# Short convolution with eight time steps by sixteen channels on the partitions

## The chip, the cores and the metric

The kernel runs on one core of a Trainium2 chip. The core has a matrix engine (TensorE, PE in the profile; PEld is its weight load), a vector engine (DVE), a scalar engine (ACT), GpSimd (POOL), a sync engine (SP) that issues most transfers, and 16 DMA engines. TensorE writes only to PSUM, and only DVE and ACT read PSUM here. The metric is the device time of one execution in microseconds; less is better.

## What is computed

Sequence length 2048, width 640, bf16 inputs. A block with a layer norm, a short convolution with four taps, a long convolution by FFT and a gate, and then a second layer norm with an MLP:

```python
k_shift = sum(k_pad[:, t:t + S, :] * shift_k[:, ks - 1 - t] for t in range(4))
kv = k_shift * v
y = irfft(rfft(kv, 2 * S) * rfft(ssm_k, 2 * S))[:S] + kv * ssm_D
h = x + layernorm(x) * y
out = h + mish(layernorm(h) @ w1 + b1) @ w2
```

## The kernel before

Each step of the work is an operation with a name, an engine (or a choice of two), operations that it depends on, and PSUM tiles that it fills or uses. The text `ORDER` (L26 on) lists all 660 names. Every engine issues its operations in the order of that list and waits only for what they depend on; `:d`, `:a` or `:p` puts an operation on DVE, ACT or POOL where it has a choice (ACT is the default for most evictions), and `@0` to `@3` gives the matmul groups one of four PSUM slots of 1024 float32 columns. A group can only start when the slot's last user has been evicted.

Channels come in five blocks m (0 to 4) of 128, in which channel = 20 d + 4 m + l, with d of 32 and l of 4. Stages, by name:

- `d_n`, `dadd`, `k1pe`, `k1ev`: load the long filter, add the skip term at time 0, transpose it 16 steps at a time.
- `s1kpe`, `s1kev`: first stage of the filter's transform, 20 pieces of 16 matmuls (L399, L400), each evicted with 1024 columns. `s2kpe`, `s2kev` (L425 with 160 columns): second stage, 22 pieces of 6 matmuls (the last of 2), which need every `s1kev` and their piece of the table (`d_g`). `sw` (L453): ten DMAs that swap partitions of the result; they need all `s2kev`.
- Short convolution. k is loaded with 16 consecutive time steps in a partition (128 partitions). `ktpe` (L344) transposes it as float32 words, which hold two channels each: 40 transposes give tiles whose partitions are 4 time steps by 32 d, for four groups of time steps. `ktev` copies them to SBUF (`kt_s`), `ktsh` (L348, POOL) makes a copy of the last group shifted by one partition of time, so that the first group can see the 16 steps before. `kspe` (L360, L361): ten groups (m, half h of the time groups) of 16 matmuls. For each l and time group, L360 multiplies the tile with a 128 x 128 banded weight, and L361 adds the reach-over: the time group before it, into the first 96 columns, since three of the four time steps of a group need taps from the group before. `kv` (L365, DVE) multiplies by v.
- The weights of that convolution: `cfpe` (L307) repeats the taps over the partitions, `coef` (L312, four casts) writes them shifted by the time step, `wsh0` to `wsh3` (L320, POOL) multiply them with a mask, five of the 20 (m, l) pairs in each, 224 columns a pair.
- `s1vpe`/`s1vev`, `s2v*pe`/`s2v*ev`: the same two stages for kv (20 pieces, then 20 pieces of L425 with 64 or 32 columns). `pr` (L464, DVE): the products in frequency. `i1pe`/`i1ev` (L485): first inverse stage, 20 pieces. `i2` (L537), `y`: second inverse stage, 16 tiles t of 128 tokens, evicted by `y`.
- `ln1`, `ln1p`, `lnx`: first layer norm of a tile (DVE statistics, POOL, then POOL or ACT). `wb`, `h`: gate and residual. `bn`, `pow`, `hc`: second layer norm. `tr` (DMA transposes, L579) or `trpe`/`trev` for the first two tiles: the normalised tile, transposed.
- MLP in five units of 2, 2, 4, 4 and 4 tiles: `m1pe` (L604, L611), `hb` (ACT, Mish), `m2pe` (L669, L677), `res` (DVE), `d_out`.

Lines L264 and L266 are the helper that all evictions go through, on ACT and on DVE.

Of the kernel before, what the change touches and what calls it, by code (L numbers as in the profile page):

```python
# [27 lines left out]
s1kpe0_3@3 k1ev1 s1kpe0_1@0 s1kev0_3 d_k1 s1kpe0_0@1 dadd2 s1kev0_1 s1kpe1_3@2 s1kev0_0:d dadd3:p d_g4 s1kpe0_2@3 k1pe2@0 s1kev0_2 dadd4:p d_g1  # L28
s1kev1_3 kz b1pe@1 k1pe4@3 k1ev2 c_b1 cfpe@2 k1pe3@1 k1ev4:a coef d_v0 s1kpe2_0@0 k1ev3 wsh1 s1kpe2_1@2 s1kev2_0 s1kpe4_3@3 d_g7 s1kev2_1:d s1kpe3_1@1
s1kev4_3 s1kpe2_2@0 wsh3 s1kpe1_0@2 s1kev3_1 d_v1 s1kev2_2:d s1kpe4_1@3 d_g2 s1kev1_0 s1kpe3_2@1 s1kev4_1:d s1kpe1_2@0 s1kev3_2 d_g6 ktpe0_0@2 wsh2  # L30
ktpe0_3 ktpe0_2 s1kev1_2 ktpe2_0@3 ktpe2_3 ktpe2_2 d_v2 ktpe2_1 ktpe0_1 ktev2 ktpe1_0@1 ktev0:a ktpe1_1 ktpe1_3 ktpe1_2 s1kpe3_3@0 d_g5 ktev1 ktsh2
s1kpe4_0@3 s1kev3_3 s1kpe1_1@2 ktsh0 s1kev4_0:d d_v3 s1kpe4_2@1 wsh0 s1kev1_1 s1kpe3_0@0 s1kev4_2:d s1kpe2_3@3 s1kev3_0 d_g3 ktpe4_0@2 ktpe4_2 ktpe4_3
s1kev2_3 ktsh1 ktpe3_0@1 ktpe4_1 ktpe3_3 ktev4 ktpe3_1 ktpe3_2 s2kpe_6@0 s2kpe_12@3 ktev3 s2kev_6 kspe0_0@2 s2kev_12 s2kpe_18@0 kv0_0 ktsh3 kspe2_0@1
s2kev_18 ktsh4 s2kpe_42@3 kv2_0 kspe3_0@2 s2kev_42 s2kpe_96@0 kv3_0 s2kpe_24@1 s2kev_96 kspe4_0@3 s2kev_24 kspe1_0@2 kv4_0 s2kpe_108@0 kspe1_1@1 kv1_0
s2kev_108 s2kpe_72@3 kspe0_1@0 d_x1 s2kev_72 kv1_1 d_x0 s2kpe_66@2 s2kpe_102@3 s2kev_66 kv0_1 kspe4_1@1 s2kev_102 s2kpe_120@2 kv4_1 kspe3_1@0
# [3 lines left out]
s1vpe0_3@1 s1vev1_2 s1vpe1_3@0 s1vev0_3:d s1vpe0_1@2 s1vev1_3 s1vpe3_0@3 s1vev0_1:d s1vpe4_1@1 s1vev3_0 s2kpe_30@0 s1vev4_1:d s2v0pe_0@2 s2kev_30
s2v0pe_48@3 s2v0ev_0 ln1_1 sw1_0 s1vpe2_0@1 s2v0pe_64@0 sw1_1 s2v0ev_48 lnx0:p s1vev2_0:d s2v0pe_112@2 sw0_0 ln1p1 s2v0ev_64 sw4_0 s2v0pe_32@3  # L40
s2v0ev_112:d s2v0pe_80@1 sw3_1 s2v0ev_32 s1vpe3_1@0 lnx1:p sw0_1 ln1_2 s1vpe4_0@2 s2v0ev_80 sw3_0 s1vpe3_3@3 sw4_1 ln1_3 s1vev3_1 ln1p2 s1vpe2_3@1
sw2_0 s1vev4_0 s1vev3_3:d sw2_1 s1vpe4_2@0 lnx2:p s1vev4_2 s2v0pe_96@3 pr1_64 ln1p3 s2v0pe_16@2 s2v0ev_96 s2v2pe_32@0 s1vev2_3:d lnx3:p s2v0ev_16
# [130 lines left out]
def kernel(  # L173
# [28 lines left out]
    cst = cpool.tile([P, 3 * P + 32], BF16, name="cst")  # L202
# [537 lines left out]
```

## Time and profile before

| what | value |
|---|---|
| median of 3 runs (lowest to highest) | 222.93 us (222.92 to 223.5) |
| profiled execution, its own time | 223.02 us |
| its span in the profile | 221.2 us |
| granted clock of TensorE | 0.999 |
| PE busy | 212.5 us, 96% |
| DVE, ACT, POOL busy | 137.6, 127.9, 62.0 us |

The span runs from the first to the last instruction; the profiled execution's own time has 1.8 us around it. In the timeline a line has a start, a length, the engine, the source line, the operation, output and input and a count of merged instructions; the brackets at the end give the idle time before it and what ended it. The chain of waits is followed back from the last instruction.

### The profile page before, as it was taken

Reading aid. Unit: us, or ns where it says so; the run is one execution under the profiler, and the core shown is the slowest. Engines: PE = TensorE matmul, PEld = TensorE weight load, DVE = VectorE, ACT = ScalarE, POOL = GpSimd, SP = SyncE. Lnnn points to the kernel's source line nnn. Section 1 sums busy time; section 2 is a strip of 40 time slices with the busy share of each in tenths; the row PEclk is TensorE's granted clock in tenths of the full one; section 3 lists DMA queues with packets and bytes.
Section 4 is the critical chain, followed back from the end, with each engine's and each line's share of the span. In section 5 each row is a group of like instructions: output and inputs, shape, how many; then the busy total and the mean of one; then the engine's idle time right before and its main releaser. Section 6 shows DMA issues by size and latency. Waiting matters only on the chain.

```text
span 221.2 us, 6309 instructions
## 1 busy us (share of the span) xinstructions
PE 212.5 (96%) x2740; PEld 156.0 (71%) x2746; DVE 137.6 (62%) x236; ACT 127.9 (58%) x175; POOL 62.0 (28%) x123
## 2 busy tenths in 40 slices
PE   7899999999879999999999999999999999999994
PEld 2899999898769998578867644444567445667663
DVE  2776899999999999899998679920002200002223
ACT  2389888999999999899753038426600257020000
POOL 5147620011870002147988655320000000000000
PEclk9999999999999999999999999999999999999999
DMA  5999994462992690833004402552001100000204
GB/s 168 393 408 416 407 403 109 166 205 87 410 409 92 207 384 9 276 127 77 0 1 27 94 0 59 124 119 59 0 3 59 59 0 3 0 0 3 89 0 148
DMA packets 19564, 30.98 MB, mean 140 GB/s; under 512 B 10705, under 2 KB 14929, under 8 KB 18769
## 3 DMA queue, kind: packets, MB, share of 16 engines
q1 hardware_dynamic: 19104, 30.46, 40.0%
q8 instruction: 21, 0.34, 0.6%
q10 hardware_dynamic: 336, 0.12, 0.2%
q14 instruction: 7, 0.05, 0.1%
q0 software_dynamic: 96, 0.00, 0.0%
HBM read 20.42 MB, written 2.62 MB: 104 GB/s over the span
## 4 chain that ended last, share of the span: by engine, by line
PE 72%; ACT 12%; DVE 6%; DMA 5%; issue 2%; SPq 1%; DVEq 0%; ACTq 0%
PE ps L669 26%; PE ps L604 26%; ACT uv L264 9%; PE ps L537 3%; DMA ks<-ks 3%; PE ps L399 3%; PE ps L425 3%; DMA ks<-in_A_ssm_k_dram 3%; PE ps L344 2%; PE ps L379 2%; DVE ks L266 2%; ACT ks L264 2%; PE ps L360 2%; DVE ra L365 1%; DVE uv L266 1%
## 5 line engine op out<-in xcount | busy, mean ns | idle before, releaser
L626 ACT ACTIVATE ks<-ps,b1s 128x512 bf16<-128x512 f32 (+1 forms) x69 | 36.2, 599 | 44.1 <-PE ps L604 35.1
L669 PE MATMUL ps<-ks 128*128 128x320 bf16 (+2 forms) x420 | 58.6, 299 | 0.0
L604 PE MATMUL ps<-G 128*128 128x512 bf16 (+1 forms) x319 | 57.2, 336 | 0.3
L669 PEld LDWEIGHTS <-ks 128*128 128x128 bf16 x420 | 40.6, 98 | 17.4 <-issue 1.3
L694 DVE TENSOR_TENSOR rb<-ps,rb 128x640 bf16<-128x640 f32 x15 | 11.8, 817 | 64.5 <-PE ps L677 52.2
L604 PEld LDWEIGHTS <-G 128*128 128x128 bf16 x325 | 31.4, 98 | 24.3 <-issue 1.1
L264 ACT CAST ks<-ps 128x960 bf16<-128x960 f32 (+3 forms) x48 | 39.3, 896 | 8.3 <-PE ps L400 5.0
L264 ACT CAST uv<-ps 128x1024 bf16<-128x1024 f32 x46 | 42.6, 1157 | 0.5 <-PE ps L485 0.4
L464 DVE TENSOR_TENSOR ks<-ks,uv 128x2048 bf16<-128x2048 bf16 x20 | 23.4, 1236 | 0.2 <-DMA ks<-ks 0.2
L425 PEld LDWEIGHTS <-G 128*128 128x128 bf16 x512 | 21.0, 96 | 3.1 <-issue 2.5
L485 PE MATMUL ps<-a_t,ks 128*128 128x128 bf16 (+1 forms) x416 | 17.1, 208 | 0.4
L485 PEld LDWEIGHTS <-ks 128*128 128x128 bf16 (+1 forms) x416 | 16.5, 114 | 1.0 <-issue 0.4
L266 DVE CAST uv<-ps 128x1024 bf16<-128x1024 f32 x14 | 16.4, 1210 | 0.2
L530 POOL TENSOR_SCALAR ra<-rb,r,nmr 128x640 bf16<-128x640 bf16 x11 | 12.5, 1133 | 9.9 <-PE ps L400 9.3
L425 PE MATMUL ps<-uv,G 128*128 128x64 bf16 (+1 forms) x384 | 12.9, 187 | 1.7 <-ACT uv L264 1.5
L550 DVE BATCH_NORM_STATS2 st<-rb 128x6 f32<-128x320 bf16 x32 | 14.0, 479 | 0.1
L516 DVE BATCH_NORM_STATS2 st<-rb 128x6 f32<-128x320 bf16 x32 | 13.7, 469 | 0.0
L365 DVE TENSOR_TENSOR ra<-ps,rb 128x1024 bf16<-128x1024 f32 x10 | 11.9, 1222 | 0.7 <-PE ps L361 0.5
L266 DVE CAST ks<-ps 128x1024 bf16<-128x1024 f32 (+2 forms) x10 | 11.3, 1160 | 1.0 <-PE ps L537 0.6
L528 ACT ACTIVATE ra<-rb,nmr,r 128x640 bf16<-128x640 bf16 x5 | 4.5, 925 | 11.9 <-POOL nmr L523 11.9
L425 PE MATMUL ps<-ks,G 128*128 128x160 bf16 x128 | 11.2, 230 | 0.1
L399 PE MATMUL ps<-cst,ra 128*64 128x128 bf16 x160 | 10.6, 219 | 0.7 <-ACT uv L264 0.5
(71 smaller groups left out, 252.7 us busy)
## 6 DMA issues: line engine op xcount, KB each, us to landing
ks<-ks SPq DMA_DIRECT2D x10, 512.0 KB, 6.3
G<-tab_g SPq DMA_DIRECT2D x8, 512.0 KB, 11.1
ks<-in_A_ssm_k_dram SPq DMA_DIRECT2D x5, 512.0 KB, 6.5
ra<-in_A_k_dram SPq DMA_DIRECT2D x4, 640.0 KB, 10.6
rb<-in_A_v_dram SPq DMA_DIRECT2D x4, 640.0 KB, 11.4
rb<-in_A_q_dram SPq DMA_DIRECT2D x4, 640.0 KB, 5.0
out_dram<-rb SPq DMA_DIRECT2D x15, 160.0 KB, 1.8
G<-in_B_w_dram SPq DMA_DIRECT2D x5, 432.0 KB, 5.9
```

Of the source, the lines that this page charges most:

```text
L264: nc.scalar.copy(o, i)
L266: nc.vector.tensor_copy(o, i)
L365: nc.vector.tensor_tensor(kv_w[:, m, :, 8 * h:8 * h + 8, :], p_.f32().rearrange("p (l t d) -> p d t l", l=4, t=8), raw_v[:, 8 * h:8 * h + ...
L399: nc.tensor.matmul(ps[0:64, dgl, :], lhs, mc, start=True, stop=True)
L425: nc.tensor.matmul(p_.f32()[:, o:o + n], g_v[:, f, :], src[:, :, f, :], start=True, stop=True)
L464: nc.vector.tensor_tensor(o, o, v, ALU.mult)
L485: nc.tensor.matmul(o, KS[r, k, b, :, l], a12[r, k, r], start=k == 0, stop=k == 1)
L516: nc.vector.bn_stats(st1[:, t, hh, :], xt(t)[:, hh * 320:(hh + 1) * 320])
L550: nc.vector.bn_stats(st2[:, t, hh, :], xt(t)[:, hh * 320:(hh + 1) * 320])
L604: nc.tensor.matmul(ph[:, o:o + w], w1[:, dc, fc * P:fc * P + P], lt[:, dc, 0:w], start=dc == 0, stop=dc == NDC - 1)
L626: nc.scalar.activation(hb[:, fc, 0:n], p_.f32()[:, i * 512:i * 512 + n], ACT.Mish, bias=b1s[:, fc:fc + 1], scale=1.0)
L669: nc.tensor.matmul(p_.f32()[:, o:o + n], lhs, w2[:, k, cols:cols + n], start=fc == 0, stop=single and fc == 13)
```

## The change

The transposes of k now give tiles whose partitions are 8 time steps by 16 channels d (a of 2 time groups, x of 2 halves of the 32 channels d), from words 20 apart instead of 10, and each needs two of the four pieces of k. The reach-over is into 48 columns (3 time steps of 16 channels). Matmuls and transposes keep their number. The taps are repeated by two matmuls over 16 partitions from a zero-padded copy (`skz`), the weights are built by five operations `wsh0` to `wsh4`, one for each block m, as two POOL instructions each (880 and 528 elements a partition instead of 1120), and the shifted copy has 1016 elements a partition instead of 508. `ORDER` is new behind `d_g1`, with 662 names.

```diff
-    mk, rep4 = cst[:, 2 * P:2 * P + 32], cst[0:32, 2 * P + 32:3 * P + 32]
-    wsh = [rw[:, i * 1120:(i + 1) * 1120].rearrange("p (g n) -> p g n", n=224) for i in range(4)]
+    mk, rep8 = cst[:, 2 * P:2 * P + 16], [cst[0:16, (2 + i) * P + 16:(3 + i) * P + 16] for i in range(2)]
+    wsh = [(rw[:, 880 * m:880 * m + 880].rearrange("p (g n) -> p g n", n=176), uv[:, 4096 * m + 3072:4096 * m + 3600].rearrange("p (g n) -> p g n", n=176)) for m in range(NDC)]
+    wsh_of = lambda m, i: wsh[m][0][:, i] if i < 5 else wsh[m][1][:, i - 5]
...
-    kt_s = [uv[:, 4096 * m:4096 * m + 2560].rearrange("p (h a t o) -> p h a t o", h=2, a=5, o=2) for m in range(NDC)]
+    kt_s = [uv[:, 4096 * m:4096 * m + 3072].rearrange("p (h a t o) -> p h a t o", h=4, a=3, o=2) for m in range(NDC)]
...
-    cf_pe = OP("cfpe", "pe", [d_cst, d_sk], psum=cf_p, emit=lambda e: nc.tensor.matmul(cf_p.f32()[:, 0:80], rep4, sk_r[:], start=True, stop=True))
+    cf_pe = OP("cfpe", "pe", [d_cst, c_skz], psum=cf_p, emit=lambda e: [nc.tensor.matmul(cf_p.f32()[:, 0:200], rep8[i], sk_z[:, :, 1 - i:6 - i], start=i == 0, stop=i == 1) for i in range(2)])
...
-            nc.vector.tensor_copy(coef[q, :, a:a + 4], cf_p.f32()[q, 0:80].rearrange("p (g j) -> p g j", j=4))
+            nc.vector.tensor_copy(coef[q, :, 2 * a:2 * a + 5], cf_p.f32()[q, 0:200].rearrange("p (g j) -> p g j", j=5))
...
-            out = wsh[l].rearrange("p g (j d) -> p (g j) d", d=32)
-            m = mk.unsqueeze(1).to_broadcast([P, 35, 32])
-            k = coef[:, l * 5:l * 5 + 5, :].rearrange("p g j -> p (g j)").unsqueeze(2).to_broadcast([P, 35, 32])
-            (nc.gpsimd if e == "pool" else nc.vector).tensor_tensor(out, m, k, ALU.mult)
+            c = coef[:, 8 * l:8 * l + 8, :].rearrange("p g j -> p (g j)")
+            for w, a, b in ((wsh[l][0], 0, 55), (wsh[l][1], 55, 88)):
+                out = w.rearrange("p g (j d) -> p (g j) d", d=16)
+                m = mk.unsqueeze(1).to_broadcast([P, b - a, 16])
+                nc.gpsimd.tensor_tensor(out, m, c[:, a:b].unsqueeze(2).to_broadcast([P, b - a, 16]), ALU.mult)
...
-                    nc.tensor.transpose(o[:, gh, a, :], raw_k.bitcast(F32)[:, a * 2 * D + m * 2 + gh:(a + 1) * 2 * D:10], ident4)
+                    c = a * 4 * D + 10 * x + 2 * m + gh
+                    nc.tensor.transpose(o[:, 2 * x + gh, a, :], raw_k.bitcast(F32)[:, c:(a + 1) * 4 * D:20], ident4)
...
-                        nc.tensor.matmul(o[:, 0:96], t[:, l // 2, a - 1 if a else 4, :, l % 2], wsh[r // 5][:, r % 5, 128:224], start=False, stop=True)
+                        nc.tensor.matmul(o[:, 0:48], t[:, 2 * x + l // 2, 0 if h else 2, :, l % 2], w[:, 128:176], start=False, stop=True)
...
-s2kev_18 ktsh4 s2kpe_42@3 kv2_0 kspe3_0@2 s2kev_42 s2kpe_96@0 kv3_0 s2kpe_24@1 s2kev_96 kspe4_0@3 s2kev_24 kspe1_0@2 kv4_0 s2kpe_108@0 kspe1_1@1 kv1_0
...
+wsh0 ktev4 ktsh0 ktpe3_3 d_v2 ktpe3_2 d_g5 s2kpe_12@2 d_v3 ktpe3_1 s2kev_12 ktev3 s2kpe_6@3 kspe2_0@0 s2kpe_42@2 s2kpe_96@1 wsh4 s2kev_6 kv2_0
+s2kev_42 ktsh3 kspe0_0@3 s2kpe_18@0 s2kev_96 d_g3 kspe3_0@2 s2kpe_24@1 ktsh4 s2kev_18 kv0_0 s2kpe_72@3 kspe4_0@0 ktsh1 kv3_0 s2kpe_102@2 s2kev_24
+s2kev_72 kspe1_0@1 s2kev_102 s2kpe_78@3 kv4_0 s2kpe_108@0 kspe0_1@2 kv1_0 s2kpe_54@1 kv0_1 s2kev_78 s2kev_108 kspe1_1@3 d_x1 s2kpe_36@0 s2kev_54
```

In the new order ACT evicts 20 of the 22 second-stage pieces of k (19 before), 13 of the first-stage pieces of v (11), 16 of its second-stage pieces (19) and 17 of the first inverse stage (16); DVE makes all five `ktev` copies (4 before). `coef` comes before the filter's `k1pe3` and `k1pe4`, `ktpe3_1` behind the first second-stage piece, `ln1_3` behind the inverse evictions. POOL's queue at the start is wsh3, wsh2, wsh1, ktsh2, wsh0, ktsh0, wsh4, ktsh3, ktsh4, ktsh1 (before: wsh1, wsh3, wsh2, ktsh2, ktsh0, wsh0, ktsh1, ktsh3, ktsh4). SP's loads keep their order up to the first DMA transposes.

More of the change, by code (lines that the diff above doesn't have):

```diff
@@ L39 @@
[L39 to L42, printed above, removed]
@@ L59 @@
-d_out5 hb4_3 d_out6 m2pe8@0 m1pe4_0@3 hb4_6 m2pe11@1 hb4_0 res11 m2pe12@3 d_out4 m2pe14@1 res9 m2pe10@2 res12 m2pe13@3 res14 res13 d_out12 d_out14
-res10 m2pe15a@1 m2pe15b@3 d_out9 d_out13 d_out10 d_out11 res15a res8 d_out15a res15b d_out8 d_out15b
+s1kpe0_3@3 k1ev1 s1kpe0_1@0 s1kev0_3 d_k1 s1kpe0_0@1 dadd2 s1kev0_1 s1kpe1_3@2 s1kev0_0:d dadd3:p d_g4 s1kpe0_2@3 k1pe2@0 s1kev0_2 dadd4:p d_g1 skz
+s1kpe1_2@1 cfpe@3 s1kev1_2 d_v0 d_g7 s1kev1_3:d k1pe3@2 coef k1ev3 k1pe4@1 b1pe@3 k1ev2:a c_b1 k1ev4 kz s1kpe1_0@2 s1kpe3_3@0 s1kpe3_2@3 s1kev1_0
@@ L200 @@
     big = ctx.enter_context(tc.tile_pool(name="big", bufs=1))
-    cst = cpool.tile([P, 3 * P + 32], BF16, name="cst")
+    cst = cpool.tile([P, 4 * P + 16], BF16, name="cst")
     ident = cpool.tile([P, P], BF16, name="ident")[:]
```

101 lines of the change are left out of this document (53 added, 48 removed).

## The prediction

> **What bounds the kernel now.** I read the page first (its head and its chain of waits), then the whole chain in order of time, then busy time by stretches, then the timeline of one engine after the other, and last the windows of single source lines.
>
> ```profile
> span 221.2 us, 6309 instructions
> ```
> ```profile
> 97.24 14.27 PE ps L604 x130
> ...
> 210.50 7.73 PE ps L669 x56
> 218.25 0.42 DVE rb L691
> ```
> ```profile
> 20.00:30.00 10.00, 10.00 (x175) 9.55 (x175) 7.70 (x7) 8.31 (x9) 5.17 (x7) 1.00 1.02 411
> 30.00:40.00 10.00, 10.00 (x181) 9.89 (x179) 9.39 (x9) 8.53 (x10) 0.60 (x2) 1.00 0.69 241
> ...
> 70.00:80.00 10.00, 10.00 (x226) 9.86 (x224) 10.00 (x10) 10.00 (x13) 0.00 (x0) 1.00 0.61 210
> ...
> 140.00:221.20 81.20, 78.01 (x498) 45.84 (x499) 14.36 (x26) 20.34 (x34) 2.61 (x6) 1.00 0.14 41
> ```
>
> The chain has two halves. From 97.24, when the first matmul of the MLP starts, it is TensorE alone up to 218.25, and 2.95 us of eviction and store follow. The change touches no matmul there, so a gain must bring 97.24 forward. Before it, a busy PE says little: the columns of the stretches (stretch, length, then PE, PEld, DVE, ACT, POOL) show DVE and ACT at 10.00 of 10 in 70 to 80, and only before 40 do both still have idle time (ACT 1.69 in 20 to 30, 1.47 in 30 to 40). ScalarE's own timeline shows where that idle time lies:
>
> ```profile
> 28.13 3.79 ACT L264 CAST ks<-ps 128x960 bf16<-128x960 f32 x4 [1.15 <-PE ps L425]
> 32.16 1.82 ACT L264 CAST ks<-ps 128x960 bf16<-128x960 f32 x2 [0.24 <-PE ps L425]
> 34.57 0.96 ACT L264 CAST ks<-ps 128x960 bf16<-128x960 f32 x1 [0.59 <-PE ps L425]
> 35.78 0.96 ACT L264 CAST ks<-ps 128x960 bf16<-128x960 f32 x1 [0.24 <-PE ps L425]
> 36.98 8.37 ACT L264 CAST ks<-ps 128x960 bf16<-128x960 f32 x10 [0.25 <-PE ps L425]
> 45.29 7.43 ACT L264 CAST uv<-ps 128x1024 bf16<-128x1024 f32 x8
> 52.58 1.00 ACT L264 CAST ks<-ps 128x960 bf16<-128x960 f32 x1
> ...
> 59.80 26.77 ACT L264 CAST uv<-ps 128x1024 bf16<-128x1024 f32 x29
> 87.00 2.08 ACT L264 CAST uv<-ps 128x1024 bf16<-128x1024 f32 x2 [0.42 <-PE ps L485]
> 89.55 6.34 ACT L264 CAST ks<-ps 128x640 bf16<-128x640 f32 x10 [0.47 <-PE ps L537]
> ```
>
> Read it as one long job: 65 evictions from 28.13 to 89.08 with 0.24 + 0.59 + 0.24 + 0.25 + 0.42 = 1.74 us of holes; the four early ones, 1.32 us, end with a second-stage matmul of the k transform (L425). DVE's job beside it ends at the same moment:
>
> ```profile
> 13.60 1.01 DVE L312 CAST coef<-ps 32x80 bf16<-32x80 f32 x4
> ...
> 27.02 2.36 DVE L266 COPY uv<-ps 128x2048 bf16<-128x2048 bf16 x2 [1.05 <-ACT ks L264]
> 29.30 3.68 DVE L365 TENSOR_TENSOR ra<-ps,rb 128x1024 bf16<-128x1024 f32 x3
> 33.44 7.18 DVE L365 TENSOR_TENSOR ra<-ps,rb 128x1024 bf16<-128x1024 f32 x6 [0.47 <-PE ps L361]
> ...
> 64.84 19.66 DVE L464 TENSOR_TENSOR ks<-ks,uv 128x2048 bf16<-128x2048 bf16 x17 [0.25 <-DMA ks<-ks]
> 84.42 4.75 DVE L266 CAST uv<-ps 128x1024 bf16<-128x1024 f32 x4
> ```
>
> So the work to shorten is ScalarE's 61 us run, and it can lose its holes, its late start, or items.
>
> **The change part by part. Reach-over matmuls.** TensorE's two rows for the wanted widths are these (first a window of L361 with its neighbours, then second-stage matmuls of 64 and of 32 columns):
>
> ```profile
> 28.47:29.26 0.79, 0.79 (x8) 0.62 (x7) 1.00 1.03 415
> ```
> ```profile
> 61.88 1.61 PE L425 MATMUL ps<-uv,G 128*128 128x64 bf16 x48 [0.28 <-ACT uv L264]
> ...
> 66.46 0.96 PE L425 MATMUL ps<-uv,G 128*128 128x32 bf16 x32 [0.28 <-ACT uv L264]
> ```
>
> Eight pairs of 128 + 96 columns take 0.79 us, 98.8 ns a pair; shared out by columns (224 of them), the 96 take 42 ns. Forty-eight columns have no row. From below the 32-column row bounds it, (0.96 - 0.17 of latency) / 32 = 25 ns, from above the 64-column one, (1.61 - 0.17) / 48 = 30 ns, with a weight load for each as here. I take 27. The saving is 80 x (42 - 27) = 1.2 us of TensorE (0.96 to 1.4), 0.12 us in each of the ten groups between 28 and 43. The weight loads stay, 160 in number. A group and one second-stage piece now take 1.21 us together, against 1.16 us of DVE for the product and some 0.84 us of ACT (8.37 / 10) for the piece, so ACT's holes of a quarter of a microsecond are this rhythm: 0.12 off halves them, and the new order, which sends two pieces between groups at places (42 and 96, 24 and 72, 78 and 108), can close them. I put the four holes at 0.05 to 0.4 together and take 0.2; the last of 0.42 stays. That is **-1.12**.
>
> **One eviction more on ACT.** Counted from the two orders, after the last first-stage eviction of k: ACT has 20 instead of 19 second-stage evictions of k, and 46 others in both (13 instead of 11 of the first stage of v, 16 instead of 19 of its second, 17 instead of 16 of the inverse). At 0.84 us: **+0.84**. DVE gets one eviction fewer there (1.16), and ln1_3 (1.1) goes behind the inverse's evictions: 2.3 us less, so DVE has room and ACT alone sets the end.
>
> **The start of that run.** TensorE does the same 40 transposes and 20 first-stage pieces before it, but two of the transposes (ktpe3_1) now stand behind the first second-stage piece.
>
> ```profile
> 19.23 3.14 PE L344 MATMUL ps<-ident,ra 128*128 128x128 f32 x24
> ```
>
> Two at 3.14 / 24 = 131 ns are 0.26 us. Against it stand a second coefficient matmul and 200 columns instead of 80, some 0.1 us. On DVE, skz and the four coefficient casts (200 elements each instead of 80) come in. 13.60 shows 0.25 us a cast; from nothing more to 2.5 times, I take +0.12 each, 0.7 us with skz. They stand where DVE waited before (1.12 us for TensorE), and coef moves ahead of k1pe3 and k1pe4, so POOL still starts at 14.5 or so:
>
> ```profile
> 12.27 1.23 DVE L266 COPY ks<-ps 128x2048 bf16<-128x2048 bf16 x1 [1.12 <-PE ps L504]
> ```
>
> Uncovered they would delay coef, and all of POOL behind it, by 0.7. The fifth transposed copy goes from ACT to DVE (1.2 us), which had 1.05 us idle at 27.02. I walked the order through to 29 with these durations, four PSUM slots and the engine order: no wait above 0.2 us stays, and the first second-stage piece starts about 0.4 earlier. **-0.4** (0.7 late to 0.6 early). The constants table grows by a quarter; first use is at 8.35, so 1 us more of landing is hidden:
>
> ```profile
> cst<-tab_cst ACTq DMA_DIRECT2D x1, 104.0 KB, 4.3
> ```
>
> **Stride of the transposes.** They now read every twentieth word (80 bytes) instead of every tenth. No row has that stride; bounds are 0 and, in proportion, twice 131 ns for 40 of them, +5.2 us before 28 on the engine that is full. I take 0, since the same number of separate words is read. The Trainium skill (SBUF — State Buffer, "Door 1: The DMA port swizzle") says that an access pays for each new 16-byte line; by that both strides pay for every word, and the sum has 0 too. No run here shows it.
>
> **POOL.** This is the part that grows most:
>
> ```profile
> 14.69 6.12 POOL L320 TENSOR_TENSOR rw<-cst,coef 128x1120 bf16<-128x1120 bf16 x3 [2.75 <-DVE coef L312]
> ...
> 29.43 1.17 POOL L348 COPY uv<-uv 128x508 bf16<-128x508 bf16 x2 [2.87 <-DVE uv L266]
> ```
>
> Weights: 4 x 1120 elements become 5 x (880 + 528) = 7040. At 2.04 us for 1120 the five are 12.8 us; a start cost in the tenth instruction lengthens it to 13.4, 2.68 for each. Shifts: 508 elements in 0.59 become 1016, 1.1 us each. POOL's queue from 14.5 is wsh3, 2, 1, ktsh2, wsh0, ktsh0, wsh4, ktsh3, 4, 1, done at about 23.6 (ktsh2), 27.4, 31.2 (ktsh3), 32.3, 33.4. By my walk TensorE wants them at 28.4, 29.8, 30.9, 32.7 and 33.8. Before, POOL waited 2.87 us for its data at 29.43; now it is level with TensorE, one wait of 0.3, which the two full PSUM slots ahead of ACT absorb: **0**. Bounds: proportional (12.8) nothing; if a run of 16 costs what a run of 32 did (35 runs in 2.04, 88 now), 5 x 5.1 us and +12.
>
> **Earlier swaps.** The swap DMAs wait for the last second-stage eviction (52.58) and keep their order:
>
> ```profile
> 53.64 10.83 SPq L453 DMA_DIRECT2D ks<-ks x10
> ```
>
> That eviction is now ACT's 24th item instead of its 27th, some 2.7 us sooner, so the products (L464) keep ahead of the inverse; DVE's room pays for the wait for the first swap. No gain by itself. SP's queue has the same loads in the same order up to the first transpose.
>
> **The MLP's start and later.** y0's group and ten y evictions on ACT follow as before (89.55), so 97.24 moves with ACT's end. The third unit's matmuls need the last of four normalised tiles, by DVE and then a DMA transpose:
>
> ```profile
> 123.31 0.44 DVE L565 TENSOR_SCALAR rw<-rb,mv,r 128x640 bf16<-128x640 bf16 x1
> ```
> ```profile
> DMA to landing us min/median/max: 2.6/2.6/4.2
> ```
> ```profile
> 128.36 0.32 PE ps L604
> ```
> ```profile
> L516 DVE BATCH_NORM_STATS2 st<-rb 128x6 f32<-128x320 bf16 x32 | 13.7, 469 | 0.0
> L544 DVE TENSOR_TENSOR ks<-ks,ra 128x640 bf16<-128x640 bf16 x16 | 7.6, 502 | 0.8 <-POOL ra L530 0.8
> ```
>
> It is done at 123.75, landed by 126.4 (127.6 with one transpose ahead in the queue), wanted at 128.36. From y0 to that tile DVE gets one ln1 more (2 x 0.47 + 0.2), one y (0.8), two wb fewer (1.0): +0.9. The slack of 0.8 to 2.0 shrinks to about 0 to 1; 0 on the path.
>
> **Sum:** -1.12 + 0.84 - 0.4 = -0.7. The profiled execution took 223.02 (span 221.2, 1.8 around it), which gives 222.3; its time lies 0.09 above the median of the runs, 222.93, so I forecast 222.2.
>
> **The rivals. The holes stay** (R1): the wait between second-stage pieces is one for PSUM slots, which the shorter matmul doesn't free. Then -1.12 becomes -0.3 and the sum is +0.1: 222.6 to 223.4. For it: DVE's 1.16 us a product is as long as TensorE's 1.21, so little is left to gain. Against: each hole names the second-stage matmul.
>
> **POOL is late** (R2, the other side): TensorE stands in front of the third group (kspe3_0) for ktsh3, with all second-stage pieces queued behind it, and ACT runs dry. It decides from the point where a wsh takes more than 2.75 us; all five stand ahead of ktsh3, so each 0.1 beyond costs 0.5. At 3.1 us ktsh3 is 5 x 0.42 = 2.1 late, of which full slots cover 0.5: +1.6 on -0.7, so 223.8; up to 226 with slower runs. For it: no slack is left, 16-long runs have no row. Against: 2062 to 2072 ns in all four before shows a rate by elements only if the run length doesn't matter. The Trainium skill (GPSIMD Engine Reference, "3.1 Elementwise — side-by-side cycle accounting") gives a two-input operation 2.6 cycles an element at 1.2 GHz; by that a wsh is an estimated 3.05 us. The row has 1.82 ns an element, below the page's 2.17, so it bears that rate out badly so far.
>
> **The transposes slow down** (R3): at +1 to +5.2 us before 28, 224 to 227.5. For it only the missing row.
>
> **More than forecast** (R4): POOL in time, start 0.6 early, all holes closed: -1.74 + 0.84 - 0.6 = -1.5, so 221.4, give or take 0.3.
>
> **How the numbers follow.** Forecast (221.7 to 222.6) 0.40, R1 0.16, R2 0.25, R3 0.07, R4 0.12. What a measurement of this kernel can't tell from no change is within 0.3% of 222.93, 222.26 to 223.60. Faster: 0.22 of the forecast, all of R4 and 0.02 of R1, 0.36. Same: 0.18 of the forecast, 0.12 of R1 and 0.03 of R2's mild end, 0.33. Slower: 0.02 of R1, 0.22 of R2 and R3, 0.31. The range of 221.3 to 224.4 leaves out a third of R4, most of R3 and the upper third of R2, 2 in 10.
>
> **What would show it.** Right: L361 spaced by 27 ns behind its partner; ACT's holes between 28 and 38 under 0.4; ACT's last inverse eviction done at 88.4; L604's first at 96.5; L320 as pairs of some 1.65 and 1.03 us, and POOL's ktsh1 over by 33.5. Wrong: PE waiting for POOL in the list of waits (none does now), L344 spaced by more than 135 ns, a wait of PE at the third unit's first matmul near 127.7, or the span after 97 longer than 121 us plus the tail.

## The result and the profile after

| what | before | after |
|---|---|---|
| median of 5 runs each (lowest to highest) | 223.00 us (222.92 to 223.50) | 224.16 us (224.12 to 224.24) |
| ratio, 95% interval | | 1.0053 (1.0042 to 1.0063) |
| profiled execution, its span | 223.02, 221.2 us | 224.23, 222.4 us |
| PE, DVE, ACT, POOL busy | 212.5, 137.6, 127.9, 62.0 us | 212.7, 139.9, 126.7, 67.8 us |

The kernel became slower by 0.5%, 1.16 us: inside the range, on the other side of no change than the forecast. Line numbers are those of each kernel: behind the change L344 is L351, L360 and L361 are L367 and L368, L264 and L266 are L266 and L268, L425 is L432, L604 and L669 are L611 and L676.

First the chain of waits of the changed kernel (start, length, work), its last part:

```profile
98.28 14.27 PE ps L611 x130
...
211.75 7.73 PE ps L676 x56
```

The MLP starts 1.04 us later than before (97.24), and from there to the last matmul it takes 121.20 us, 0.2 more than before. So the loss lies ahead of 98. ScalarE's timeline divides it:

```profile
30.52 12.64 ACT L266 CAST ks<-ps 128x960 bf16<-128x960 f32 x15 [1.44 <-PE ps L432]
43.28 1.01 ACT L266 CAST uv<-ps 128x1024 bf16<-128x1024 f32 x1
...
51.58 38.65 ACT L266 CAST uv<-ps 128x1024 bf16<-128x1024 f32 x42
90.59 6.34 ACT L266 CAST ks<-ps 128x640 bf16<-128x640 f32 x10 [0.36 <-PE ps L544]
```

The long run of evictions has 66 items and no marked hole, from 30.52 to 90.23: 59.71 us, where before it was 60.95. The change shortened this run, by more than was forecast: -1.24. But the run starts at 30.52 instead of 28.13: **+2.39**. The two make +1.15 at the end of the run, which is the loss. Now TensorE's stretches of transposes ahead of that start, by windows of their line (start and end, length, PE busy, PEld busy, then the granted clock, the DMA share and GB/s), and one of the reach-over's line:

```profile
20.38:23.45 3.07, 3.07 (x18) 2.88 (x18) 1.00 1.02 415
27.58:30.02 2.44, 2.44 (x14) 2.24 (x14) 1.00 1.01 417
```
```profile
31.21:31.85 0.64, 0.64 (x8) 0.50 (x7) 1.00 1.02 421
```

A transpose takes 3.07 / 18 = 171 ns, where 24 took 3.14 us before (131): 40 ns more for each of 40, 1.6 us on an engine that is full. A pair of a full and a reach-over matmul takes 0.64 / 8 = 80 ns instead of 98.8: 1.5 us less for the 80 pairs. What else is new ahead of the run stands in DVE's timeline and in TensorE's list of waits (waited for, us in total, times, longest):

```profile
13.27 1.60 DVE L315 CAST coef<-ps 32x200 bf16<-32x200 f32 x4 [0.77 <-PE ps L310]
14.89 2.36 DVE L268 COPY ks<-ps 128x2048 bf16<-128x2048 bf16 x2
```
```profile
PE ps L386 <- DMA ks<-in_A_ssm_k_dram: 1.4, 2, 0.9
...
PE ps L406 <- DVE ks L268: 0.8, 1, 0.8
```

The four casts of the taps take 1.60 us (1.01 before), and the eviction behind them (`k1ev3`) is one that a first-stage matmul (L406) waits 0.8 us for. POOL does not appear in that list. Its timeline:

```profile
15.00 1.66 POOL L324 TENSOR_TENSOR rw<-cst,coef 128x880 bf16<-128x880 bf16 x1 [2.86 <-PE ps L386]
16.63 1.07 POOL L324 TENSOR_TENSOR uv<-cst,coef 128x528 bf16<-128x528 bf16 x1
17.66 1.66 POOL L324 TENSOR_TENSOR rw<-cst,coef 128x880 bf16<-128x880 bf16 x1
...
32.12 2.98 POOL L355 COPY uv<-uv 128x1016 bf16<-128x1016 bf16 x3 [1.30 <-DVE uv L268]
```

A block's weights come every 2.66 us, and before its last three copies POOL itself waits 1.30 us for data.

### The profile page after: what moved, and what is told of

It is laid out like the page before. It is cut to its first block, busy times and chain, and to the rows that moved or that the text cites. A ratio compares the mean times of both kernels' runs of the same rounds, so it can differ in the third digit from the quotient of the medians.

```text
span 222.4 us, 6332 instructions
## 1 busy us (share of the span) xinstructions
PE 212.7 (96%) x2747; PEld 156.5 (70%) x2747; DVE 139.9 (63%) x239; ACT 126.7 (57%) x175; POOL 67.8 (30%) x128
## 2 busy tenths in 40 slices
DMA packets 19547, 31.01 MB, mean 139 GB/s; under 512 B 10688, under 2 KB 14912, under 8 KB 18752
## 4 chain that ended last, share of the span: by engine, by line
PE 78%; ACT 11%; DVE 4%; DMA 3%; issue 2%; POOL 0%; SPq 0%; DVEq 0%; ACTq 0%
PE ps L676 26%; PE ps L611 26%; ACT uv L266 9%; PE ps L492 6%; PE ps L432 4%; PE ps L351 3%; PE ps L544 3%; PE ps L406 3%; DMA ks<-in_A_ssm_k_dram 3%; ACT ks L266 2%; PE ps L367 2%; DVE ks L268 2%; PE ps L618 1%; PE ps L684 1%; PE ps L407 1%
## 5 line engine op out<-in xcount | busy, mean ns | idle before, releaser
L676 PE MATMUL ps<-ks 128*128 128x320 bf16 (+2 forms) x420 | 58.4, 299 | 0.0
L611 PE MATMUL ps<-G 128*128 128x512 bf16 (+1 forms) x325 | 57.5, 337 | 0.0
L676 PEld LDWEIGHTS <-ks 128*128 128x128 bf16 x420 | 40.6, 98 | 17.2 <-issue 1.3
L611 PEld LDWEIGHTS <-G 128*128 128x128 bf16 x325 | 31.4, 98 | 24.6 <-issue 1.4
L266 ACT CAST ks<-ps 128x960 bf16<-128x960 f32 (+3 forms) x48 | 39.6, 896 | 12.1 <-PE ps L407 9.9
L266 ACT CAST uv<-ps 128x1024 bf16<-128x1024 f32 x46 | 42.7, 1098 | 0.2
L432 PEld LDWEIGHTS <-G 128*128 128x128 bf16 x512 | 21.1, 96 | 2.5 <-issue 0.9
L528 POOL TENSOR_SCALAR ve<-mv 128x1 f32<-128x1 f32 x16 | 4.2, 260 | 48.1 <-DVE mv L524 47.4
L268 DVE CAST uv<-ps 128x1024 bf16<-128x1024 f32 x14 | 16.6, 1212 | 0.1
L432 PE MATMUL ps<-uv,G 128*128 128x64 bf16 (+1 forms) x384 | 12.7, 187 | 1.0 <-ACT uv L266 0.9
L535 ACT ACTIVATE ra<-rb,nmr,r 128x640 bf16<-128x640 bf16 x6 | 5.5, 924 | 14.2 <-POOL nmr L530 11.6
L268 DVE CAST ks<-ps 128x1024 bf16<-128x1024 f32 (+2 forms) x10 | 11.2, 1126 | 1.1 <-PE ps L432 0.6
L406 PE MATMUL ps<-cst,ra 128*64 128x128 bf16 x160 | 11.0, 219 | 0.7 <-DVE uv L268 0.3
L432 PE MATMUL ps<-ks,G 128*128 128x160 bf16 x128 | 11.3, 230 | 0.3 <-DVE ks L268 0.2
```

The source lines that it names most:

```text
L266: nc.scalar.copy(o, i)
L268: nc.vector.tensor_copy(o, i)
L406: nc.tensor.matmul(ps[0:64, dgl, :], lhs, mc, start=True, stop=True)
L432: nc.tensor.matmul(p_.f32()[:, o:o + n], g_v[:, f, :], src[:, :, f, :], start=True, stop=True)
L611: nc.tensor.matmul(ph[:, o:o + w], w1[:, dc, fc * P:fc * P + P], lt[:, dc, 0:w], start=dc == 0, stop=dc == NDC - 1)
L676: nc.tensor.matmul(p_.f32()[:, o:o + n], lhs, w2[:, k, cols:cols + n], start=fc == 0, stop=single and fc == 13)
```

## The experiments

Each run has its own runs of the kernel before beside it, on the same chip (medians of 222.88 to 223.26); ratios are to those. A difference in us between two kernels of different sittings is uncertain by some of that spread, and a trace shows one execution out of several.

### The step of the transposes

**The changed kernel with ten words, the kernel before with twenty.** In both the transposes read other words of k than the ones wanted.

```diff
-                    c = a * 4 * D + 10 * x + 2 * m + gh
-                    nc.tensor.transpose(o[:, 2 * x + gh, a, :], raw_k.bitcast(F32)[:, c:(a + 1) * 4 * D:20], ident4)
+                    c = a * 4 * D + D + 10 * x + 2 * m + gh
+                    nc.tensor.transpose(o[:, 2 * x + gh, a, :], raw_k.bitcast(F32)[:, c:c + 1271:10], ident4)
```

> The changed kernel, but the 40 transposes of k read words 10 apart again (other words than the right ones, as many of them, from the same pieces of k). Theory A (the stride costs): L351 goes from 171-175 ns apart to 131, 40 x 43 = 1.7 us less before the second stage, whose first matmul comes at 28.3 instead of 30.0; time 222.3 to 222.7. Rival B (POOL was level, and is the bound as soon as TensorE comes earlier): the first matmul of the second stage comes earlier as well, but a wait of PE for the shifted copies of POOL appears at the third group, and 223.2 to 223.7 remain. Rival C (the order, not the stride): L351 stays above 160 ns and 224.1 stays.

```diff
-                    nc.tensor.transpose(o[:, gh, a, :], raw_k.bitcast(F32)[:, a * 2 * D + m * 2 + gh:(a + 1) * 2 * D:10], ident4)
+                    nc.tensor.transpose(o[:, gh, a, :], raw_k.bitcast(F32)[:, 4 * D + 10 * (a % 2) + m * 2 + gh:8 * D:20], ident4)
```

> The kernel before, but its transposes read words 20 apart (other words than the right ones, as many of them). A: L344 from 131 to 174 ns, +1.7 us before the second stage where TensorE is full, and nothing behind it gives it back: 224.3 to 224.8. C: no more than 223.3.

The changed kernel with ten words: 222.98 us, ratio 0.9988 (0.9963 to 1.0012), 1.2 below the changed kernel and between the ranges of A and B. The kernel before with twenty: 224.45, ratio 1.0062 (1.0040 to 1.0085), as A says. The second is the cleaner proof, for only the words that the transposes read differ. The weight loads of the transposes before and in that run (duration ns as lowest, median, highest, then first and last start), then its ScalarE timeline and its chain of waits:

```profile
L344 PEld LDWEIGHTS ps<-ident,ra x40: 194/209/218, 19.2 to 27.2; 128*128 128x128 f32 x40
```
```profile
L344 PEld LDWEIGHTS ps<-ident,ra x40: 234/272/273, 19.2 to 28.8; 128*128 128x128 f32 x40
```
```profile
29.71 3.79 ACT L264 CAST ks<-ps 128x960 bf16<-128x960 f32 x4 [1.97 <-PE ps L425]
33.75 1.82 ACT L264 CAST ks<-ps 128x960 bf16<-128x960 f32 x2 [0.25 <-PE ps L425]
```
```profile
98.83 14.27 PE ps L604 x130
```

The run of evictions starts 1.58 us later than before (28.13), keeps its holes, and the MLP starts 1.59 later (97.24): what is lost ahead of the second stage is carried whole to the end. In the first run only part of the gain arrived in some executions; its profiled one (223.88, the slowest of 222.38 to 223.88) shows a wait for it, in the timelines of DVE and ACT:

```profile
44.86 0.89 DVE L523 BATCH_NORM_STATS2 st<-rb 128x6 f32<-128x320 bf16 x2 [1.01 <-DMA rb<-in_A_q_dram]
```
```profile
48.26 2.14 ACT L266 CAST uv<-ps 128x1024 bf16<-128x1024 f32 x2 [1.01 <-PE ps L407]
```

Earlier by a microsecond and more, DVE reaches `ln1_2` before the first q load has landed, and all evictions behind it are late: the next wait behind the one removed. The run with the q loads exchanged, below, tests that.

**A table of steps.** The same line, with a step of its own for each of ten groups of four transposes (other words of k), in two kernels.

```diff
-                    c = a * 4 * D + 10 * x + 2 * m + gh
-                    nc.tensor.transpose(o[:, 2 * x + gh, a, :], raw_k.bitcast(F32)[:, c:(a + 1) * 4 * D:20], ident4)
+                    if 2 * m + a == 0:
+                        nc.tensor.transpose(o[:, 2 * x + gh, a, :], raw_k.bitcast(F32)[:, 2 * x + gh + 2476:2476 + 2 * x + gh + 128:1], ident4)
...
+                    elif 2 * m + a == 8:
+                        nc.tensor.transpose(o[:, 2 * x + gh, a, :], raw_k.bitcast(F32)[:, 2 * x + gh + 1270:1270 + 2 * x + gh + 2541:20], ident4)
...
```

> The changed kernel with ten strides among its 40 transposes, four each: 1, 2, 4, 5, 8, 10, 12, 16, 20 and 40 words (other words than the right ones). If every word on a 16-byte line of its own costs the same, 4 to 40 words are level and only 1 and 2 are cheaper; then 10 against 20 in the two kernels is something else. If the cost follows the bytes spanned, it grows from step to step up to 20 and 40. Weight load rows: 209 ns at 10 and 276 at 20 are known.

> The changed kernel, its ten groups of four transposes each with a step of their own: 15, 18, 19, 21, 22, 24, 25, 28, 30 and 36 words of four bytes (other words of k than the ones wanted). In e3_strides only 20 words was slow (weight load 272 ns, matmul 323) and 2 to 16 and 40 lay at 194 to 217 and 276 to 291. Theory (a narrow property of 80 bytes): 19 and 21 lie near 200 and 280, as does all else here. Rival (a band around 20, or every step from 18 to 36): 19 and 21, or 18 to 36, lie at 270 and 320 as well.

Median lengths of the weight load and the matmul of a transpose, in ns (four transposes a step, one execution of each kernel):

| step, words | 1 | 2 | 4 | 5 | 8 | 10 | 12 | 15 | 16 | 18 |
|---|---|---|---|---|---|---|---|---|---|---|
| weight load | 146 | 206 | 212 | 202 | 194 | 203 | 217 | 212 | 196 | 210 |
| matmul | 273 | 282 | 286 | 280 | 277 | 283 | 291 | 286 | 277 | 283 |

| step, words | 19 | 20 | 21 | 22 | 24 | 25 | 28 | 30 | 36 | 40 |
|---|---|---|---|---|---|---|---|---|---|---|
| weight load | 211 | 272 | 254 | 236 | 197 | 200 | 207 | 202 | 209 | 194 |
| matmul | 288 | 323 | 310 | 298 | 274 | 280 | 282 | 280 | 283 | 276 |

The rows of 10, 20 and 40 words in the first kernel, and of 19 and 21 in the second (duration ns as lowest, median, highest, then first and last start):

```profile
L361 PEld LDWEIGHTS ps<-ident,ra x4: 195/203/209, 21.0 to 21.6; 128*128 128x128 f32 x4
...
L367 PEld LDWEIGHTS ps<-ident,ra x4: 237/272/272, 26.7 to 27.2; 128*128 128x128 f32 x4
...
L369 PEld LDWEIGHTS ps<-ident,ra x4: 193/194/225, 27.3 to 27.7; 128*128 128x128 f32 x4
```
```profile
L355 PEld LDWEIGHTS ps<-ident,ra x4: 200/211/223, 21.9 to 24.2; 128*128 128x128 f32 x4
...
L357 PEld LDWEIGHTS ps<-ident,ra x4: 238/254/254, 24.3 to 24.7; 128*128 128x128 f32 x4
```

Neither reading foresaw this: it is not 80 bytes alone (21 and 22 words are slow too, by less), and there is nothing of it on the other side (19) or from 24 up. The change happened to choose the worst of the 20 steps tried, by 55 ns or more over 17 of them. Why these three, the runs do not tell; the start word is not it, for three kernels whose transposes start at different words (this one, the changed kernel, and the kernel before with twenty) give 272 to 276 at a step of 20. The Trainium skill (SBUF — State Buffer, "Door 1: The DMA port swizzle") says that each access to a new 16-byte line pays a penalty; by that a step of 2 words, with two on each line, is cheaper than one of 4, and every step from 4 words up costs the same. The rows agree for 15 of the 18 steps from 4 up (194 to 217 ns), but not for 20, 21 and 22, nor for 2, which costs 206: the measurement decides.

**The right words, as two-byte values.** Eighty transposes of two-byte values, 80 bytes apart, in place of forty of four-byte words; the copy keeps the two halves of a word apart. The second kernel also issues the first q load ahead of the second.

```diff
-                o = p_.f32().rearrange("p (h a t) -> p h a t", h=4, a=2)
+                o = p_.b16().rearrange("p (h a o t) -> p h a o t", h=4, a=2, o=2)
...
-                    c = a * 4 * D + 10 * x + 2 * m + gh
-                    nc.tensor.transpose(o[:, 2 * x + gh, a, :], raw_k.bitcast(F32)[:, c:(a + 1) * 4 * D:20], ident4)
+                    c = a * 8 * D + 20 * x + 4 * m + 2 * gh
+                    for u in range(2):
+                        nc.tensor.transpose(o[:, 2 * x + gh, a, u, :], raw_k[:, c + u:(a + 1) * 8 * D:40], ident)
```

> The changed kernel with the right words of k, transposed as two-byte values: 80 transposes with a step of 40 values (80 bytes, as now) in place of 40 of four-byte words; the transposed copy holds the two halves of a word one after the other. The first-stage transposes of the profile, two-byte ones too, take 1.17 to 1.22 us for 16, 75 ns each, with a step of 32 bytes. Theory (the price of 80 bytes is one of four-byte words, or of the load's length): 80 x 75 = 6.0 us in place of 40 x 171 = 6.85, the second stage of k starts 0.5 to 0.9 earlier, 223.3 to 223.7. Rival (a step of 80 bytes slows every weight load, here 80 of them, by some 40 ns): 80 x 115 = 9.2 us, 2.3 more than now, 226 to 226.8.

> As e15_two_byte_transposes, and the first load of q issued ahead of the second; it computes the whole reference. If the two-byte transposes take 75 ns each, the time is that of e10_step10_x0_first (222.49) with 0.8 us more of transposes: 222.9 to 223.3. If they take 115 ns, 226 or more, and the q load makes no difference.

Measured: 226.07, ratio 1.0143 (1.0103 to 1.0184), and 225.65, ratio 1.0118 (1.0098 to 1.0138). The first time is the rival's, the second nearly; the traces say otherwise. The line's group and two waits of the first kernel (its profiled execution, 228.15, was its slowest):

```profile
L352 PEld LDWEIGHTS <-ra x80: 140/147/168, 20.9 to 30.9; 128*128 128x128 bf16 x80
```
```profile
PE ps L407 <- issue: 1.1, 1, 1.1
...
PE ps L433 <- issue: 1.0, 2, 0.9
```

And of the second, the first transposes in its chain of waits and ACT's timeline:

```profile
20.26 2.40 PE ps L352 x36
```
```profile
29.11 12.54 ACT L266 CAST ks<-ps 128x960 bf16<-128x960 f32 x15 [1.09 <-PE ps L433]
```

A two-byte load with this step takes 147 ns, less than any four-byte load with a step of two words or more, and as long as the first-stage transposes' two-byte loads 32 bytes apart (L386, 149 in the changed kernel); a transpose takes 2.40 / 36 = 67 ns, and not the rival's 115. So the extra price of 80 bytes was paid by four-byte words alone. In the second kernel the run of evictions does start earlier than in the changed one (30.52); in the slow execution of the first it starts at 31.01, behind 1.0 us in which TensorE stood among the transposes without a wait that the profile shows. Most of the time went later: TensorE stands up to 1.1 us at a time in that way, at places far behind the transposes, and the second kernel's run of evictions takes 61.40 us (29.11 to 90.51) instead of 59.71. The kernel has 74 instructions more; whether that is the cause was not tried.

### The narrow reach-over alone

The changed kernel with 96 columns again; the further columns come from weights that belong elsewhere.

```diff
-                        nc.tensor.matmul(o[:, 0:48], t[:, 2 * x + l // 2, 0 if h else 2, :, l % 2], w[:, 128:176], start=False, stop=True)
+                        nc.tensor.matmul(o[:, 0:96], t[:, 2 * x + l // 2, 0 if h else 2, :, l % 2], w[:, 80:176], start=False, stop=True)
```

> The changed kernel with its reach-over matmuls 96 columns wide again (the other 48 columns from weights that belong elsewhere). A pair goes from 81 ns back to 98, 1.4 us more of TensorE between 31 and 46. If the narrower matmul is worth its whole saving, 225.2 to 225.6 and holes of 0.2 in ACT's run of second-stage evictions; if evictions set that stretch anyway, 224.1 to 224.4.

225.09 us, ratio 1.0089 (1.0065 to 1.0114): 0.93 above the changed kernel, just below the range of the first reading. ScalarE's timeline:

```profile
30.92 13.43 ACT L266 CAST ks<-ps 128x960 bf16<-128x960 f32 x15 [1.44 <-PE ps L432]
...
52.92 38.61 ACT L266 CAST uv<-ps 128x1024 bf16<-128x1024 f32 x42
```

The first 15 evictions take 13.43 us instead of 12.64, and the whole run 60.61 instead of 59.71. Here the narrow matmul is worth 0.9 us of time, of the 1.5 that it saves TensorE.

### The order alone, and the order taken away

The old convolution in the new order (without the names `skz` and `wsh4`, which it lacks), and then the same with the first q load ahead:

> The convolution of before (four steps by 32 channels, words 10 apart, 96 columns) in the new order. If the new order by itself is worth something, below 222.6; if its beginning costs (0.7 to 0.9 us before the second stage in the run with 10 words, with the coefficients ahead of the filter's copies) and its later part gains nothing, 223.3 to 224.2: the wider reach-over (1.2) in place of the dearer stride (1.7).

```diff
-s2kev_72 kspe1_0@1 s2kev_102 s2kpe_78@3 kv4_0 s2kpe_108@0 kspe0_1@2 kv1_0 s2kpe_54@1 kv0_1 s2kev_78 s2kev_108 kspe1_1@3 d_x1 s2kpe_36@0 s2kev_54
-s2kpe_120@2 d_x0 s2kev_36 kspe4_1@1 kv1_1 s2kpe_84@3 kv4_1 s2kev_120 s2kev_84 kspe3_1@0 kv3_1 s2kpe_126@2 s1vpe0_0@1 s2kev_126 s2kpe_114@3 s1vev0_0
+s2kev_72 kspe1_0@1 s2kev_102 s2kpe_78@3 kv4_0 s2kpe_108@0 kspe0_1@2 kv1_0 s2kpe_54@1 kv0_1 s2kev_78 s2kev_108 kspe1_1@3 d_x0 s2kpe_36@0 s2kev_54
+s2kpe_120@2 d_x1 s2kev_36 kspe4_1@1 kv1_1 s2kpe_84@3 kv4_1 s2kev_120 s2kev_84 kspe3_1@0 kv3_1 s2kpe_126@2 s1vpe0_0@1 s2kev_126 s2kpe_114@3 s1vev0_0
```

> The convolution of before in the order of after (as e6_old_conv_new_order, 223.17), with the first q load issued ahead of the second; it computes the whole reference. Theory (the order of after is worth something and the late q load takes it back in part of the executions): 222.3 to 222.7, ratio to before 0.997 to 0.999, with less spread than e6's 222.53 to 223.83. Rival (the order of after is worth nothing by itself): 222.9 to 223.2.

223.17, ratio 1.0011 (0.9998 to 1.0024), and 222.79, ratio 1.0000 (0.9987 to 1.0012); each lies between its two readings. By the medians the order by itself is worth nothing that can be measured, though its executions spread by more than a microsecond (222.37 to 223.83) and both profiled ones (222.53 and 222.50) are among the fastest. Of the second, ACT's timeline and DVE's:

```profile
28.20 4.55 ACT L263 CAST ks<-ps 128x960 bf16<-128x960 f32 x5 [0.88 <-PE ps L424]
33.00 8.67 ACT L263 CAST ks<-ps 128x960 bf16<-128x960 f32 x10 [0.25 <-PE ps L424]
...
49.87 38.63 ACT L263 CAST uv<-ps 128x1024 bf16<-128x1024 f32 x42
```
```profile
12.74 1.01 DVE L311 CAST coef<-ps 32x80 bf16<-32x80 f32 x4 [0.62 <-PE ps L306]
13.88 2.35 DVE L265 COPY ks<-ps 128x2048 bf16<-128x2048 bf16 x2
```

The order closes most of the early holes even with 96 columns (0.25 and one of 0.26 later are left): 60.30 us for the run, which starts no earlier than before (28.20; in the first of the two 28.13, as before).

The other way round is the new convolution in the order of before, each of the five `wsh` at the place where its block needs it. Here the word step is 10, and k is loaded in two halves so that the words are the right ones:

```diff
-    d_k = [load(f"d_k{a}", raw_k[:, a * 4 * D:(a + 1) * 4 * D], flat(A_k)[:, a * 4 * D:(a + 1) * 4 * D]) for a in range(4)]
+    d_k = [load(f"d_k{a}", raw_k.rearrange("p (x t c) -> p x t c", x=2, t=NT)[:, a % 2, 8 * (a // 2):8 * (a // 2) + 8, :], flat(A_k).rearrange("p (t x c) -> p x t c", t=NT, x=2)[:, a % 2, 8 * (a // 2):8 * (a // 2) + 8, :]) for a in range(4)]
...
-                    c = a * 4 * D + 10 * x + 2 * m + gh
-                    nc.tensor.transpose(o[:, 2 * x + gh, a, :], raw_k.bitcast(F32)[:, c:(a + 1) * 4 * D:20], ident4)
+                    c = 2560 * x + 1280 * a + 2 * m + gh
+                    nc.tensor.transpose(o[:, 2 * x + gh, a, :], raw_k.bitcast(F32)[:, c:c + 1271:10], ident4)
```

> The convolution of the split load (eight by sixteen, words 10 apart, 48 columns) in the order of before, with skz and a fifth weight operation put in. If the narrow reach-over and the old order are both good, second stage from 27.8, the four holes of 0.24 to 0.59 in ACT's run halved, 222.0 to 222.6. If POOL's 7.2 us more are not covered in an order made without them, PE waits for POOL at the first groups and 223.5 or more.

225.12, ratio 1.0099 (1.0077 to 1.0120). TensorE's list of waits and ACT's timeline:

```profile
PE ps L368 <- POOL uv L355: 1.4, 1, 1.4
```
```profile
34.10 1.82 ACT L266 CAST ks<-ps 128x960 bf16<-128x960 f32 x2 [1.65 <-PE ps L432]
```

Here POOL is late, as the second reading has it: the third group waits 1.4 us for its shifted copy and ScalarE runs dry for 1.65. With the five `wsh` at these places the order of before does not cover POOL, and the new one does; other places in the old order were not tried.

### The right words by another load

The same split load in the new order, and then with the first q load ahead:

> The changed kernel with k loaded so that the two halves of the channel groups lie apart (runs of 640 bytes; d = 16 x + d' instead of 2 d' + x), so that eight time steps by sixteen channels are words 10 apart. It computes the reference. Theory A (20 words apart is what costs): L351 at 131 ns, second stage from 28.6, 222.4 to 222.9, as with the wrong words. Rival (the shorter runs slow the load of k, 2.6 MB at the full rate of the DMA engines): TensorE waits for k at 20 to 22, and 223.3 or more stays.

> The split load in the new order, with the loads d_x0 and d_x1 exchanged, since ln1_2 on DVE needs d_x0 and stood still for it in the run with 10 words (1.0 us hole of ACT at 47.2). If that wait is what holds the gain back, 0.5 to 1.0 us below the split load alone; if not, the same within 0.3.

223.78, ratio 1.0045 (1.0011 to 1.0078), from 222.45 to 225.68; and 223.43, ratio 1.0036 (1.0015 to 1.0057), 0.35 less, between the two readings. The weight loads of the transposes are back at 208 and 209 ns, but k now comes in pieces of 640 bytes. The transfers of the first 40 us, in the changed kernel and in the first of the two, and that one's TensorE waits (its profiled execution, 225.05, is a late one):

```profile
DMA packets 3606, 12.44 MB, mean 311 GB/s; under 512 B 640, under 2 KB 896, under 8 KB 3601
```
```profile
DMA packets 7189, 12.36 MB, mean 309 GB/s; under 512 B 656, under 2 KB 5008, under 8 KB 7184
```

```profile
PE ps L351 <- DMA ra<-in_A_k_dram: 1.4, 1, 1.4
```

Twice the packets, and a transpose waits 1.4 us for its piece of k. In the profiled execution of the second (223.36) no transpose waits for k; there the long filter's load is waited for (L386, 0.8), and the run of evictions starts at 29.69, 0.98 later than with ten words and whole rows (28.71, below). So what the transposes gain the split load gives back, in whole or in large part, but at which transfer differs from execution to execution.

### What is left at the start

Three more kernels with one exchange or two in the order. With ten words (other words of k) and the first q load ahead:

> The changed kernel with transposes that step by 10 words and read other words of k than the ones wanted (as in e1_step10), and the first load of q (d_x0) issued ahead of the second (d_x1). In e1_step10 DVE waited 1.01 us for the first q tile at 44.86 and ScalarE then stood 1.01 us at 48.26. Theory (the stride and the q load are separate costs in series): the hole at 48 is gone, the MLP's first matmul comes about 1.0 earlier than e1's 97.95, and the time is 222.0 (ratio to before 0.995 to 0.997). Rival (the load is bound by the same transfer queue in either order, or DVE's slack absorbs it): the hole stays or shifts and the time is 222.7 to 223.1.

222.49, ratio 0.9978 (0.9967 to 0.9990), the only run whose interval lies below 1, though not as far down as the theory's 222.0. ACT's timeline:

```profile
28.71 12.57 ACT L266 CAST ks<-ps 128x960 bf16<-128x960 f32 x15 [0.87 <-PE ps L432]
...
49.71 38.65 ACT L266 CAST uv<-ps 128x1024 bf16<-128x1024 f32 x42
```

The hole at 48 is gone. The run is 59.65 us long, as in the changed kernel, and starts 1.81 earlier. Beside the old convolution in the same order (28.20, 60.30) it starts 0.51 later. The longer casts of the taps (1.59 us against 1.01) fit that in size, for here TensorE waits 0.7 us for the `k1ev3` behind them, and there 0.2:

```profile
PE ps L406 <- DVE ks L268: 0.7, 1, 0.7
```
```profile
PE ps L398 <- DVE ks L265: 0.2, 1, 0.2
```

Then `coef` and `k1ev3` exchanged, in that kernel and in the changed one:

```diff
-s1kpe1_2@1 cfpe@3 s1kev1_2 d_v0 d_g7 s1kev1_3:d k1pe3@2 coef k1ev3 k1pe4@1 b1pe@3 k1ev2:a c_b1 k1ev4 kz s1kpe1_0@2 s1kpe3_3@0 s1kpe3_2@3 s1kev1_0
+s1kpe1_2@1 cfpe@3 s1kev1_2 d_v0 d_g7 s1kev1_3:d k1pe3@2 k1ev3 coef k1pe4@1 b1pe@3 k1ev2:a c_b1 k1ev4 kz s1kpe1_0@2 s1kpe3_3@0 s1kpe3_2@3 s1kev1_0
```

> As e10_step10_x0_first (other words of k), and the eviction k1ev3 on DVE stands ahead of the four coefficient casts. Theory (the casts, 1.6 us, hold back the eviction that TensorE waits 0.7 us for): that wait goes, the second stage of k starts some 0.7 earlier (ScalarE's run from about 28.3), POOL starts 1.2 later (at about 15.8) and is in time still: 0.3 to 0.7 below e10. Rival (POOL has no slack left): TensorE waits for POOL's shifted copies or weights in front of a group, up to 1.2 us, and the time is that of e10 or up to 0.5 above it.

> The changed kernel, only the eviction k1ev3 on DVE standing ahead of the four coefficient casts instead of behind them. Theory (the casts' 1.6 us make TensorE wait 0.7 us at 16 and this is carried to the end): the wait PE <- DVE at the first stage goes, and the time is 0.3 to 0.7 below after's 224.16, 223.5 to 223.9. Rival (POOL, which starts 1.2 us later, has no slack, or TensorE's early wait is made up for before 30): no better than 224.1, with a wait of TensorE for POOL in the list.

223.73, ratio 1.0041 (1.0026 to 1.0056), 1.2 above the run without it; and 224.78, ratio 1.0097 (1.0074 to 1.0120), 0.6 above the changed kernel. Both readings missed. TensorE's list of waits of the second:

```profile
PE ps L511 <- DVE coef L315: 1.8, 1, 1.8
```

TensorE does not wait for POOL (0.2 us once in the first of the two), but for the casts themselves: `b1pe@3` (L511) takes the PSUM slot that `cfpe@3` filled, and stands in TensorE's queue until the last cast has emptied it. TensorE waits 0.7 or 0.8 us behind the casts where they are and 1.8 where they were put, so the place chosen is the better of the two. Another PSUM slot for `b1pe` was not tried.

## Why the prediction was wrong, step by step

| step | predicted | measured |
|---|---|---|
| stride of the transposes | 0 (0 to +5.2) | +1.6 |
| rest of the start of ACT's run | -0.4 | about +0.8 |
| holes and one eviction more | -1.12 + 0.84 = -0.28 | -1.24 |
| MLP's start after that, and later | 0 | +0.1 |
| sum | -0.7 | +1.2 |

**The step that failed is "Stride of the transposes: 0".** "The same number of separate words is read" was the reason for that value, and the table of steps shows that the number of words does not set the price. One word apart is cheap, two to 19 are level, and 20 is 69 ns of weight load above 10. The bounds were right (1.6 lies between 0 and 5.2), the choice between them was not: no row had the step, and the value taken was the lower bound. The chance of 0.07 for the third rival, "The transposes slow down", had "only the missing row" for it. That rival is what happened; its sign, "L344 spaced by more than 135 ns", is there with 171. The kernel before with twenty words proves it alone, with +1.55 of time. The 224.16 lies at the low end of the rival's 224 to 227.5, which is partly chance: by the prediction's own sum +1 makes 223.2 and not 224, and the rest of the start added to it. It is luck, too, that the time lies inside the range: its upper part stood there for a late POOL, and it left out "most of R3".

**The rest of the start** was to be 0.4 earlier and was later by some 0.8. The walk's 0.4 is not there even with the old convolution, which in the new order starts the run at 28.13 and 28.20. The casts were costed at 0.25 + 0.12 each, 1.48 together, and took 1.60: the size was near. Wrong was the cover: they were put "where DVE waited before". `k1ev3` stands behind them in both orders, but before, three first-stage pieces came ahead of the one that takes the PSUM slot that it empties, and in the new order the next piece (`s1kpe1_0@2`) takes it. (It is `cfpe` that moved ahead of both `k1pe3` and `k1pe4`; `coef` stands behind `k1pe3` as before, and POOL started at 15.00, not at 14.5.) Old and new convolution in one order differ by 0.5 us at the start of the run. In the profiled execution TensorE also waited 1.4 us for the long filter's load (L386), 0.9 more than before. Beside the run with ten words and the q load ahead, where that wait is 0.4, it begins the piece behind `k1ev3` 0.27 us later (16.17 against 15.90), so about 0.3 of it got through. With the transposes' 1.6 this makes the 2.39, to within 0.1.

**Holes.** The mechanism was right: the pair shortened by 19 ns (15 predicted), the four early holes are gone. The last one of 0.42, which was to stay, went as well, and with the item more the rest of the run grew by 0.5 instead of 0.84 (59.71 us without holes, against 60.95 - 1.74 = 59.21 for the 65). By the run with 96 columns 0.9 us of the 1.24 is the narrow matmul; by the old convolution the new order alone already brings 0.65 (60.30), which leaves 0.6 for it. With a step of ten words and the q load ahead the time is 222.49, 0.3 above the forecast of 222.2, by two errors that cancel: there the run's -1.30 (59.65) makes up for a start that is 0.58 later, not 0.4 earlier.

**POOL.** 2.66 us for a block's weights (2.68 predicted), below the 2.75 from which R2 decides, and no wait of TensorE for POOL. That holds for the new order only: the order of before gives the 1.4 us that the rival describes. `ktsh1` was over at 35.1 instead of 33.5, because its data came later, not POOL. The Trainium skill's 2.6 cycles an element (GPSIMD Engine Reference, "3.1 Elementwise — side-by-side cycle accounting") gave an estimated 3.05 us for a block; both rows give less, and 352 elements more cost 0.59 us, 1.7 ns each.

**MLP.** The third unit's first matmul starts at 129.40, 1.04 later than before, as the first one does: its tile's transpose stayed hidden, as argued.

## What to carry to other kernels

When an edit changes the step with which an operand is read and no row of the profile has that step, its cost is unknown, and 40 instructions on a full engine make a microsecond of a few tens of nanoseconds. Where nothing but the two bounds is known, the lower one is no forecast: give the slower end a chance that fits what is not known, or measure the step first. A reason such as "the same number of separate words" is no row. And a cost taken to be hidden by an idle stretch has to be checked against what the new order puts behind it, and against the PSUM slot that it holds.

## What was not expected of the hardware

The weight load of a four-byte transpose takes 194 to 217 ns at any step tried from 2 to 40 words, except 20 (272), 21 (254) and 22 (236); with one word it takes 146. The two-byte one takes 147 at 80 bytes. What singles out 80 to 88 bytes stays open. No kernel here computes the whole reference and is faster than the one before: the nearest, the old convolution in the new order with the first q load ahead, is level with it (ratio 1.0000).
